# One-hot comparison of the token lists: 16-bit operands contiguous in the innermost dimension

## The chip, the cores and the metric

The kernel runs on one core of a Trainium2 chip. The metric is the time of one execution on the device, in microseconds (us); of several executions the median is given.

## What is computed

The program is a block of attention with a memory, a dense feed-forward layer and a mixture of 8 experts. The part around the change is the last one (the reference, cut):

```python
def _moe2_ref(x, w_gate, w1, w2):          # x: 2304 tokens x 512
    N, D = x.shape
    E = w_gate.shape[1]                    # 8 experts
    cap = N // E                           # 288 tokens each
    flat = (x @ w_gate).flatten()
    order = np.argsort(-flat)
    for idx in order:                      # best (token, expert) pair first
        tok, e = int(idx) // E, int(idx) % E
        if assigned[tok] >= 0 or counts[e] >= cap:
            continue
        assigned[tok] = e
        counts[e] += 1
    for e in range(E):
        mask = assigned == e
        h = np.maximum(x[mask] @ w1[e], 0.0)
        out[mask] = h @ w2[e]
```

Each expert thus gets exactly 288 tokens, and the kernel needs, for each expert, the list of its tokens' numbers, to gather their rows and later to scatter the results.

## The kernel before

**Stages.** Attention runs first (to about 370 us of the trace), interleaved with the first feed-forward pass; two more feed-forward passes follow (to about 728 us); then come the experts (class `Moe`). The routing decides one expert per phase: `phase` picks the expert that is full first, with a search of two times three stages (`search`). Each stage compares all tokens with 64 or 32 thresholds on VectorE (L847), counts by 18 matmuls on TensorE (L858), turns the counts into flags on VectorE (`fl`, L860), multiplies once more (L863) and reads the next base on VectorE (L867). After a phase the position of each of the expert's tokens is known (`self.pos`, `self.mem`), the expert's number goes to SyncE, which loads its weights (`wraw`, L1063), ScalarE and GpSimd split the weights into two parts (`convert`: L1073, and L1075 on GpSimd, whose two inputs and output lie in SBUF), and `lists` makes the list of tokens.

**The list (`lists`, L987).** Token n is row n mod 128, column t = n div 128 of an array of 128 x 18. A token's position among the 288 is cut into three thirds of 96 (`CW`): `j` is the third, `rb` the place in it plus 1, or 0 if the token is not the expert's. `rb` lies in `bank`, a tile of PSUM that holds most small arrays of the routing. L1006 compares, in two operations of 9 columns (`CUTS[3]` is 2), `rb` with the numbers 1 to 96 in `slot`, and writes the one-hot array `oh`, 16-bit, in which for each column t the 96 places follow one another. For each t a matmul (L1011) takes 128 places of `oh` as its weights (the last 32 belong to the next column or to the zeroed end, and their results are not read) and adds to 128 x 6 sums of token numbers in PSUM (`rs`, a single buffer that search and lists share). L1014 and L1016 make the index `idx`, and GpSimd gathers the rows in three indirect DMAs (`gather`, L1082).

**Order.** The instructions of TensorE go in program order, written out by hand with generators: `mlps` yields after each matmul of the experts, and `routes` is resumed between them after a count of such yields (`GAPS`). The other engines' order is chosen by a planner that works with estimated times. `lists` is itself a generator: it says before each piece whether VectorE ("v") or TensorE ("p") comes next, and `spare` (L973) resumes it at fixed places of the next phase's search: one "v" piece after each stage's comparisons, one "p" piece after a stage's last VectorE operation. For the list made during the third phase (`QUICK`) it is run through at once, and for the first list and the last two it is run to its end by `finish` (L1048), which gives `GAPS[8]` = 48 resumptions to other matmuls ahead of the "p" piece where there are such. TensorE first works on expert 0 after `LEAD` = 12 resumptions of the routing, that is after the second phase's search.

**Constants.** `slot` is an iota of 96 numbers made at the very start on GpSimd (L737, through `const`, L717). `open` (L760, in the timeline near 370 us) makes two zeroed buffers `oh` of 1760 elements on GpSimd (L770), used in turn.

Of the kernel before, what the change touches and what calls it, by code (L numbers as in the profile page):

```python
# [11 lines left out]
BF16 = mybir.dt.bfloat16  # L12
AF = mybir.ActivationFunctionType
OP = mybir.AluOpType
# [665 lines left out]
NE = 8  # L680
CAP = NT // NE
NTT = NT // 128
FE = 1024
KE = FE // 128
CW = CAP // 3
# [3 lines left out]
CUTS = (2, 2, 2, 2)  # L689
# [7 lines left out]
class Moe:  # L697
# [12 lines left out]
    def __init__(self, tc, pool):  # L710
        nc = self.nc = tc.nc
        self.tc = tc
        G, V = nc.gpsimd, nc.vector

        def const(shape, pattern, base, cm, name, dt=F32):
            t_ = pool.tile(shape, dt, name=name)
            G.iota(t_, pattern=pattern, base=base, channel_multiplier=cm, allow_small_or_imprecise_dtypes=True)  # L717
            return t_

        self.jt, self.jones, self.base8 = [], [], []  # L720
        for n, u in enumerate(self.UNITS):
            ts, os = [], []
            for r, st, o in zip(self.RS, self.ST, self.BASE):
                t_ = const([128, r], [[st, r]], o, 0, f"jt{n}_{st}")
                if u != 1.0:
                    V.tensor_scalar(t_, t_, u, None, op0=OP.mult)
                ts.append(t_)
                os.append(pool.tile([128, 128], BF16, name=f"jo{n}_{st}"))
                G.memset(os[-1], 0.0)
                G.memset(os[-1][0:r], st * u)  # L730
            self.jt.append(ts)
            self.jones.append(os)
            b_ = pool.tile([128, NE], F32, name=f"base{n}")
            V.memset(b_, -u * (self.ST[0] + self.ST[1] + 1))
            self.base8.append(b_)
        self.w8 = const([128, NE], [[-1, NE]], NE, 0, "w8")
        self.slot = const([128, CW], [[1, CW]], 1, 0, "slot", BF16)  # L737
        self.j3 = const([128, 3], [[1, 3]], 0, 0, "j3")
        tp = self.tp = pool.tile([128, NTT, 2], F32, name="tp")
        G.iota(tp[:, :, 0], pattern=[[128, NTT]], base=0, channel_multiplier=0, allow_small_or_imprecise_dtypes=True)  # L740
        G.iota(tp[:, :, 1], pattern=[[0, NTT]], base=0, channel_multiplier=1, allow_small_or_imprecise_dtypes=True)
        self.ones = pool.tile([128, 128], BF16, name="ones")
        V.memset(self.ones, 1.0)
        self.tri = pool.tile([128, 128], BF16, name="tri")
        G.affine_select(out=self.tri, in_=self.ones, pattern=[[1, 128]], compare_op=OP.is_gt, fill=0.0, base=0,
                        channel_multiplier=-1)
        self.later = pool.tile([128, 2, NTT], F32, name="later")
        V.memset(self.later, 1.0)
        V.memset(self.later[:, :, 0:1], 0.0)

        self.ab = [pool.tile([128, 2, NTT + 1], BF16, name=f"ab{i}") for i in range(2)]
        for t_ in self.ab:
            V.memset(t_, 0.0)

        self.room = pool.tile([128, NE], F32, name="room0")
        V.memset(self.room, float(CAP))
        self.code = pool.tile([128, NTT], F32, name="code0")
        V.memset(self.code, 0.0)

    def open(self, ctx, lg):  # L760

        tc, self.lg = self.tc, lg
        self.rt = ctx.enter_context(tc.tile_pool(name="mrt", bufs=2, reuse_waits="tile"))
        self.ri = ctx.enter_context(tc.tile_pool(name="mri", bufs=5, reuse_waits="tile"))
        kept = ctx.enter_context(tc.tile_pool(name="mrk", bufs=1, reuse_waits="tile"))

        def full(name, w):
            ts = [kept.tile([128, w], BF16, name=f"{name}{i}") for i in range(2)]
            for t_ in ts:
                tc.nc.gpsimd.memset(t_, 0.0)  # L770
            return itertools.cycle(ts)

        self.cmps, self.ohs, self.fls = full("cmp", 64 * (NTT + 1)), full("oh", CW * NTT + 128 - CW), full("fl", NE)
        self.p1 = ctx.enter_context(tc.tile_pool(name="mop1", bufs=1, space=PSUM, reuse_waits="tile"))


        bank, self.at = self.p1.tile([128, 512], F32, name="bank"), 0
        V = tc.nc.vector

        def small(*shape, dt=F32, at=None):  # L780
            n = 1
            for x in shape:
                n *= x
            o = self.at if at is None else at
            if at is None:
                self.at += n
            t_ = bank[:, o:o + n]
            if dt != F32:
                t_ = t_.bitcast(dt)
            if len(shape) == 2:  # L790
                t_ = t_.rearrange("p (a b) -> p a b", a=shape[0])
            return t_

        wide = self.at
        self.wv = small(NTT, NE)
        self.jh = small(NTT, 3, at=wide)
        (self.m, self.mw, self.lw, self.ac, self.px1, self.pos, self.take, self.mem,
         self.rb) = (small(NTT) for _ in range(9))
        self.key, self.hi, self.lo = (small(NTT, dt=I32) for _ in range(3))
        self.mg = small(2, NTT)  # L800
        self.cnt = small(2, NE)
        self.v, self.fe, self.nd, self.w8p = (small(NE) for _ in range(4))
        self.pens = [small(NE) for _ in range(2)]
        self.j3p, self.fmp, self.idf = small(3), small(1), small(3)
        assert self.at <= 512
        V.tensor_copy(self.w8p, self.w8)
        V.tensor_copy(self.j3p, self.j3)
        V.memset(self.pens[0], 0.0)
        self.pen = self.pens[0]
        self.stores, self.turn, self.ready, self.done, self.xs, self.hs = [], 0, [], 0, {}, {}  # L810
        self.split = {}
# [12 lines left out]
    def t18(self, nm, dt=F32):  # L824
        return self.rt.tile([128, NTT], dt, name=nm)
# [161 lines left out]
    def lists(self, i, raws):  # L987

        nc, V, two, t18 = self.nc, self.nc.vector, self.rt, self.t18
        yield "v"  # L990
        j, r, pos, rb, jh = t18("j"), t18("r"), self.pos, self.rb, self.jh
        V.tensor_scalar(j, pos, float(CW), None, op0=OP.is_ge)
        V.scalar_tensor_tensor(j, pos, float(2 * CW), j, op0=OP.is_ge, op1=OP.add)
        V.scalar_tensor_tensor(r, j, -float(CW), pos, op0=OP.mult, op1=OP.add)
        V.scalar_tensor_tensor(rb, r, 1.0, self.mem, op0=OP.add, op1=OP.mult)
        V.tensor_tensor(jh, j[:, :, None].to_broadcast([128, NTT, 3]),
                        self.j3p[:, None, :].to_broadcast([128, NTT, 3]), op=OP.is_equal)
        rhs = two.tile([128, NTT, 3, 2], BF16, name="rhs")
        V.tensor_tensor(rhs, jh[:, :, :, None].to_broadcast([128, NTT, 3, 2]),
                        self.tp[:, :, None, :].to_broadcast([128, NTT, 3, 2]), op=OP.mult)  # L1000
        wide = next(self.ohs)
        oh = wide[:, 0:CW * NTT].rearrange("p (t c) -> p t c", c=CW)
        n = NTT // CUTS[3]
        for t0 in range(0, NTT, n):
            yield "v"
            V.tensor_tensor(oh[:, t0:t0 + n], rb[:, t0:t0 + n, None].to_broadcast([128, n, CW]),  # L1006
                            self.slot[:, None, :].to_broadcast([128, n, CW]), op=OP.is_equal)
        yield "p"
        ps = self.p1.tile([128, 3, 2], F32, name="rs")
        for t in range(NTT):  # L1010
            nc.tensor.matmul(ps.rearrange("p a b -> p (a b)"), wide[:, CW * t:CW * t + 128],  # L1011
                             rhs[:, t].rearrange("p a b -> p (a b)"), start=(t == 0), stop=(t == NTT - 1))
        yield "v"
        V.tensor_reduce(self.idf[0:CW], ps[0:CW], axis=mybir.AxisListType.X, op=OP.add)  # L1014
        idx = self.ri.tile([CW, 3], I32, name="idx")
        V.tensor_copy(idx, self.idf[0:CW])  # L1016
        self.ready.append((self.split[i], idx, self.gather(idx)))
        if i == 0:
            with self.tc.issue_after(self.got):
                self.convert(i, raws[:3])  # L1020
            self.raws = raws[3:]
# [303 lines left out]
```

## Time and profile before

| | |
|---|---|
| time, median of 3 runs | 1027.81 us (1027.31 to 1028.85) |
| the profiled execution | 1039.62 us, its span 1037.9 us |
| TensorE (PE) busy | 941.3 us |
| VectorE (DVE) busy | 653.6 us |
| ScalarE (ACT) busy | 553.4 us |
| GpSimd (POOL) busy | 548.6 us |
| granted TensorE clock, mean | 0.960 of full |

The span goes from the first to the last instruction of the profiled execution. PEld is TensorE's loading of weights, which overlaps its matmuls. A row of a timeline gives the start and the time taken in us, the engine, the line, the operation, what it writes and reads, how many such in a row, and in brackets how long the engine had been idle before and what ended that.

### The profile page before, as it was taken

What the parts mean: (1) busy time and instruction counts of PE and PEld (TensorE: products, weight loads), DVE (VectorE), ACT (ScalarE), POOL (GpSimd) and SP (SyncE); (2) the same over time, 40 slices, a digit from 0 to 9 for tenths busy, and PEclk for the clock granted to TensorE, in tenths of its full rate; (3) what the DMA queues carried; (4) which work ended last, traced back from release to release, by engine and by line L of the source; (5) the groups of instructions that cost most, each with busy time, mean ns of one, the idle gap of its engine ahead of it and who ended that gap; (6) DMA issues with size and microseconds to landing.
All of it is one profiled execution on the core that took longest, in us unless ns stands there. A gap on an engine that the chain in (4) does not pass through costs nothing.

```text
span 1037.9 us, 19748 instructions
## 1 busy us (share of the span) xinstructions
PE 941.3 (91%) x7017; PEld 869.5 (84%) x7017; DVE 653.6 (63%) x1919; ACT 553.4 (53%) x1370; POOL 548.6 (53%) x555
## 2 busy tenths in 40 slices
PE   5787879999999989999999999999489898889996
PEld 4665768988899979999999999977388888889996
DVE  6899888788888727357426952326767677664110
ACT  6778878888888735344322333432343344335531
POOL 5666776667657546334322121211664876577841
PEclk8879889999999999999999999999699999999999
DMA  6445736364635277769684233101553355437410
GB/s 154 111 120 145 195 88 174 76 185 106 174 81 151 63 234 225 230 213 310 196 271 176 73 132 110 57 26 47 199 179 109 109 196 191 149 92 235 174 31 24
DMA packets 150723, 150.75 MB, mean 145 GB/s; under 512 B 71640, under 2 KB 122840, under 8 KB 150496
## 3 DMA queue, kind: packets, MB, share of 16 engines
q1 hardware_dynamic: 147552, 140.05, 44.1%
q0 software_dynamic: 3072, 9.44, 3.0%
q8 instruction: 55, 0.90, 0.4%
q14 instruction: 44, 0.36, 0.1%
HBM read 111.69 MB, written 37.77 MB: 144 GB/s over the span
## 4 chain that ended last, share of the span: by engine, by line
PE 61%; DVE 13%; issue 7%; DMA 6%; ACT 6%; POOL 3%; SPq 2%; another core or an unknown queue 0%; POOLq 0%; DVEq 0%; ACTq 0%
PE ph L1091 11%; PE ph L46 7%; PE ph L48 6%; PE ph L47 6%; PE py L46 4%; PE py L47 4%; PE py L48 4%; PE ps L313 3%; PE ps L218 2%; DMA xf<-x_d 2%; PE ps L272 2%; DVE cmp L847 2%; DMA wraw<-in_moe_w_dram 2%; PE rs L858 1%; PE ps L132 1%
## 5 line engine op out<-in xcount | busy, mean ns | idle before, releaser
L490 POOL TENSOR_TENSOR gf<-r 128x384 f32<-128x384 f32 (+1 forms) x108 | 87.4, 810 | 201.3 <-ACT r L488 191.1
L1075 POOL TENSOR_TENSOR wsp<-wraw,wsp 128x1024 fp32r<-128x1024 f32 x64 | 150.9, 2386 | 42.7 <-ACT wsp L1073 42.4
L27 DVE TENSOR_TENSOR gs<-gf,gs 128x384 fp32r<-128x384 f32 (+1 forms) x108 | 65.4, 605 | 92.0 <-ACT gs L26 91.4
L1091 PE MATMUL ph<-xs,wsp 128*128 128x288 f32 x768 | 120.0, 307 | 0.0
L1091 PEld LDWEIGHTS ph<-xs,wsp 128*128 128x128 f32 x768 | 107.9, 194 | 9.4 <-issue 9.2
L1091 PE MATMUL ph<-hs,wsp 128*128 128x288 f32 x768 | 114.5, 303 | 0.0
L247 POOL TENSOR_SCALAR P<-P,R,og 128x128 f32<-128x128 f32 (+2 forms) x144 | 100.3, 711 | 22.6 <-DVE R L245 18.4
L1091 PEld LDWEIGHTS ph<-hs,wsp 128*128 128x128 f32 x768 | 105.7, 191 | 0.7 <-DVE hs L1115 0.4
L1073 ACT ACTIVATE wsp<-wraw 128x1024 fp32r<-128x1024 f32 x64 | 64.2, 1051 | 52.4 <-DMA wraw<-in_moe_w_dram 31.4
L488 ACT ACTIVATE r<-ph 128x384 f32<-128x384 f32 (+1 forms) x108 | 48.6, 450 | 77.3 <-PE ph L48 76.1
L241 ACT ACTIVATE P<-P,R 128x128 f32<-128x128 f32 (+2 forms) x144 | 83.4, 581 | 9.3 <-DVE R L229 7.4
L26 ACT ACTIVATE gs<-gf 128x384 fp32r<-128x384 f32 (+1 forms) x108 | 52.5, 486 | 57.8 <-POOL gf L490 49.5
L46 PE MATMUL ph<-xt,win 128*128 128x384 f32 x240 | 81.3, 339 | 0.0
L47 PE MATMUL ph<-xt,win 128*128 128x384 f32 x240 | 80.8, 337 | 0.0
L48 PE MATMUL ph<-xt,win 128*128 128x384 f32 x240 | 80.7, 336 | 0.0
L46 PE MATMUL ph<-xs,win 128*128 128x288 f32 x192 | 64.6, 336 | 10.7 <-ACT r L488 7.9
L272 PE MATMUL ps<-ident,P 128*128 128x128 f32 x320 | 60.6, 296 | 8.3 <-POOL P L247 2.5
L47 PE MATMUL py<-gs,wout 128*128 128x384 f32 x192 | 64.9, 339 | 0.0
L27 DVE TENSOR_TENSOR ptb<-ps,ptb 128x384 fp32r<-128x384 f32 (+3 forms) x128 | 59.2, 464 | 8.1 <-ACT ptb L26 6.4
L48 PE MATMUL py<-gs,wout 128*128 128x384 f32 x192 | 64.0, 337 | 0.0
L229 DVE CUSTOM_DVE_ANT_0 P<-ps,maskw 128x128 f32<-128x128 f32 (+3 forms) x128 | 58.6, 484 | 8.0 <-PE ps L218 4.5
L46 PE MATMUL py<-gs,wout 128*128 128x384 f32 x192 | 63.5, 338 | 0.0
(264 smaller groups left out, 2595.1 us busy)
## 6 DMA issues: line engine op xcount, KB each, us to landing
wraw<-in_moe_w_dram SPq DMA_DIRECT2D x32, 1024.0 KB, 8.0
xt<-xs_d SPq DMA_DIRECT2D x12, 1536.0 KB, 7.1
x_d<-xo SPq DMA_DIRECT2D x32, 288.0 KB, 3.8
xf<-x_d SPq DMA_DIRECT2D x32, 288.0 KB, 3.9
xs_d<-xs SPq DMA_DIRECT2D x8, 1152.0 KB, 6.8
raw<-in_moe_w_in_dram SPq DMA_DIRECT2D x16, 512.0 KB, 5.3
raw<-in_moe_w_out_dram SPq DMA_DIRECT2D x16, 512.0 KB, 4.4
yp<-yo SPq DMA_DIRECT2D x32, 144.0 KB, 4.5
```

The costliest lines, as they stand in the source:

```text
L27: (eng or nc.vector).tensor_tensor(lo, src, hi.bitcast(F32), op=OP.subtract)
L46: nc.tensor.matmul(out, lhi, rhi, start=start, stop=False)
L47: nc.tensor.matmul(out, lhi, rlo, start=False, stop=False)
L48: nc.tensor.matmul(out, llo, rhi, start=False, stop=stop)
L229: nc.vector.tensor_tensor_reduce(out=pw, in0=ps[:, 0:W[u]], in1=maskw[:, 512 - 128 * t:640], op0=OP.add, op1=OP.min, scale=-0.125, scalar= ...
L241: nc.scalar.activation(pw, pw, AF.Exp, bias=R[:, 0, u:u + 1], scale=-1.0, accum_out=R[:, 1, u:u + 1])
L247: nc.gpsimd.tensor_scalar(PP[n][w], PP[n][w], R[:, 2, w:w + 1], og9[:, hp, w:w + 1], op0=OP.mult, op1=OP.mult)
L272: nc.tensor.transpose(tr[:, 128 * i:128 * i + 128], P[:, 128 * i:128 * i + 128], ident)
L490: nc.gpsimd.tensor_tensor(gf, r, r, op=OP.mult)
L1073: nc.scalar.activation(w[:, 0, hs], raw[:, hs], AF.Copy)
L1075: eng.tensor_tensor(w[:, 1, hs], raw[:, hs], w[:, 0, hs].bitcast(F32), op=OP.subtract)
L1091: nc.tensor.matmul(out, l[a], r[b], start=i + p == 0, stop=i == n - 1 and p == 2)
```

## The change

`rb` becomes a 16-bit tile in SBUF. `slot` becomes a constant of 96 x 18 16-bit elements, in which each number stands 18 times in a row; it is made in `open`. `oh` is laid out as 128 places of 18 columns, with one buffer in place of two, and is filled by one comparison in place of two: 96 x 18 elements with the columns innermost, so that all three operands step by one element there. `lists` gives back control once less. The matmul of column t takes as weights the elements t, t + 18, t + 36, ... of `oh`, 36 bytes apart.

```diff
--- before.py
+++ after.py
@@ -734,7 +734,6 @@
             V.memset(b_, -u * (self.ST[0] + self.ST[1] + 1))
             self.base8.append(b_)
         self.w8 = const([128, NE], [[-1, NE]], NE, 0, "w8")
-        self.slot = const([128, CW], [[1, CW]], 1, 0, "slot", BF16)
         self.j3 = const([128, 3], [[1, 3]], 0, 0, "j3")
         tp = self.tp = pool.tile([128, NTT, 2], F32, name="tp")
         G.iota(tp[:, :, 0], pattern=[[128, NTT]], base=0, channel_multiplier=0, allow_small_or_imprecise_dtypes=True)
@@ -764,13 +763,16 @@
         self.ri = ctx.enter_context(tc.tile_pool(name="mri", bufs=5, reuse_waits="tile"))
         kept = ctx.enter_context(tc.tile_pool(name="mrk", bufs=1, reuse_waits="tile"))
 
-        def full(name, w):
-            ts = [kept.tile([128, w], BF16, name=f"{name}{i}") for i in range(2)]
+        def full(name, w, n=2):
+            ts = [kept.tile([128, w], BF16, name=f"{name}{i}") for i in range(n)]
             for t_ in ts:
                 tc.nc.gpsimd.memset(t_, 0.0)
             return itertools.cycle(ts)
 
-        self.cmps, self.ohs, self.fls = full("cmp", 64 * (NTT + 1)), full("oh", CW * NTT + 128 - CW), full("fl", NE)
+        self.slot = kept.tile([128, CW, NTT], BF16, name="slot")
+        tc.nc.gpsimd.iota(self.slot, pattern=[[1, CW], [0, NTT]], base=1, channel_multiplier=0,
+                          allow_small_or_imprecise_dtypes=True)
+        self.cmps, self.ohs, self.fls = full("cmp", 64 * (NTT + 1)), full("oh", 128 * NTT, 1), full("fl", NE)
         self.p1 = ctx.enter_context(tc.tile_pool(name="mop1", bufs=1, space=PSUM, reuse_waits="tile"))
 
 
@@ -988,7 +990,7 @@
 
         nc, V, two, t18 = self.nc, self.nc.vector, self.rt, self.t18
         yield "v"
-        j, r, pos, rb, jh = t18("j"), t18("r"), self.pos, self.rb, self.jh
+        j, r, rb, pos, jh = t18("j"), t18("r"), t18("rb", BF16), self.pos, self.jh
         V.tensor_scalar(j, pos, float(CW), None, op0=OP.is_ge)
         V.scalar_tensor_tensor(j, pos, float(2 * CW), j, op0=OP.is_ge, op1=OP.add)
         V.scalar_tensor_tensor(r, j, -float(CW), pos, op0=OP.mult, op1=OP.add)
@@ -998,17 +1000,13 @@
         rhs = two.tile([128, NTT, 3, 2], BF16, name="rhs")
         V.tensor_tensor(rhs, jh[:, :, :, None].to_broadcast([128, NTT, 3, 2]),
                         self.tp[:, :, None, :].to_broadcast([128, NTT, 3, 2]), op=OP.mult)
-        wide = next(self.ohs)
-        oh = wide[:, 0:CW * NTT].rearrange("p (t c) -> p t c", c=CW)
-        n = NTT // CUTS[3]
-        for t0 in range(0, NTT, n):
-            yield "v"
-            V.tensor_tensor(oh[:, t0:t0 + n], rb[:, t0:t0 + n, None].to_broadcast([128, n, CW]),
-                            self.slot[:, None, :].to_broadcast([128, n, CW]), op=OP.is_equal)
+        wide = next(self.ohs).rearrange("p (c t) -> p c t", t=NTT)
+        yield "v"
+        V.tensor_tensor(wide[:, 0:CW], rb[:, None, :].to_broadcast([128, CW, NTT]), self.slot, op=OP.is_equal)
         yield "p"
         ps = self.p1.tile([128, 3, 2], F32, name="rs")
         for t in range(NTT):
-            nc.tensor.matmul(ps.rearrange("p a b -> p (a b)"), wide[:, CW * t:CW * t + 128],
+            nc.tensor.matmul(ps.rearrange("p a b -> p (a b)"), wide[:, :, t],
                              rhs[:, t].rearrange("p a b -> p (a b)"), start=(t == 0), stop=(t == NTT - 1))
         yield "v"
         V.tensor_reduce(self.idf[0:CW], ps[0:CW], axis=mybir.AxisListType.X, op=OP.add)
```

## Rows read from the trace of the kernel before

**Rows 1.** Page, part 1: busy us, share of the span, instructions of each engine.
```profile
PE 941.3 (91%) x7017; PEld 869.5 (84%) x7017; DVE 653.6 (63%) x1919; ACT 553.4 (53%) x1370; POOL 548.6 (53%) x555
```

**Rows 2.** Stages: length; PE, PEld, DVE, ACT, POOL busy (x); PEclk, DMA share, GB/s.
```profile
728.00:750.00 22.00, 7.81 (x139) 5.49 (x138) 15.75 (x52) 6.78 (x8) 16.62 (x9) 0.61 0.67 230
750.00:1038.00 288.00, 260.70 (x2438) 250.18 (x2438) 148.73 (x551) 117.29 (x209) 179.19 (x104) 0.97 0.40 134
```

**Rows 3.** Chain that ended last, list 0: start us, us, what.
```profile
728.97 1.94 DVE oh L1006 x2
...
730.96 0.42 PE rs L1011 x10
...
731.76 0.22 DVE la L877
```

**Rows 4.** Timeline of PE, then of POOL, at list 1.
```profile
767.84 0.36 PE L1011 MATMUL rs<-rhs,oh 128*128 128x6 bf16 x8 [1.59 <-DVE oh L1006]
...
764.99 9.36 POOL L1075 TENSOR_TENSOR wsp<-wraw,wsp 128x1024 fp32r<-128x1024 f32 x4 [7.40 <-ACT wsp L1073]
```

**Rows 5.** Tile oh: count, duration ns min/median/max, first and last start, forms.
```profile
L1011 PEld LDWEIGHTS <-oh x144: 95/96/101, 730.0 to 945.6; 128*128 128x128 bf16 x144
...
L1006 DVE TENSOR_TENSOR oh<-bank,slot x16: 1046/1048/1049, 728.9 to 942.9; 128x864 bf16<-128x864 f32 x16
```

**Rows 6.** Timeline: weight loads of list 0, comparisons of list 1.
```profile
730.96 0.32 PEld L1011 LDWEIGHTS <-oh 128*128 128x128 bf16 x10 [0.70 <-DVE oh L1006]
...
766.74 2.01 DVE L1006 TENSOR_TENSOR oh<-bank,slot 128x864 bf16<-128x864 f32 x2
```

**Rows 7.** DVE: a form's busy us, mean ns; a line's ns, min/median/max.
```profile
L27 DVE TENSOR_TENSOR xs<-tr,xs 128x288 fp32r<-128x288 f32 x32 | 13.8, 452 | 22.2 <-ACT xs L26 22.2
...
L38 DVE TENSOR_SCALAR gf<-r x20: 387/692/991, 30.8 to 417.6; 128x512 int32<-128x512 int32 x20
```

**Rows 8.** Loads of four-byte weights by form: count, busy us, mean ns, idle before.
```profile
L664 PEld LDWEIGHTS pr<-two,lt 128*128 128x128 f32 x36 | 5.6, 189 | 0.3
...
L652 PEld LDWEIGHTS pr<-ys,wgs 128*16 128x16 f32 x48 | 4.4, 94 | 6.1 <-DVE ys L27 2.3 <-ACT ys L26 1.4 <-ACT yr L675 0.5
```

**Rows 9.** Timeline of DVE and POOL near 69 us; durations of L177.
```profile
69.50 1.78 DVE L177 SCALAR_TENSOR_TENSOR qp<-nq,e 128x640 f32<-128x640 f32 x1
...
69.05 1.54 POOL L163 TENSOR_TENSOR vt<-nv,vt 128x640 fp32r<-128x640 f32 x1
...
L177 DVE SCALAR_TENSOR_TENSOR qp<-nq,e x16: 811/826/2131, 8.7 to 339.3; 128x640 f32<-128x640 f32 x16
```

**Rows 10.** POOL from 750 to 945 us by line: busy us, mean ns, idle before.
```profile
L1075 POOL TENSOR_TENSOR wsp<-wraw,wsp 128x1024 fp32r<-128x1024 f32 x44 | 103.7, 2386 | 39.7 <-ACT wsp L1073 39.6
```

**Rows 11.** Timeline of DVE and POOL at lists 3 and 5.
```profile
837.37 1.05 DVE L1006 TENSOR_TENSOR oh<-bank,slot 128x864 bf16<-128x864 f32 x1
...
836.38 4.77 POOL L1075 TENSOR_TENSOR wsp<-wraw,wsp 128x1024 fp32r<-128x1024 f32 x2 [2.18 <-ACT wsp L1073]
...
905.74 1.05 DVE L1006 TENSOR_TENSOR oh<-bank,slot 128x864 bf16<-128x864 f32 x1
...
905.07 4.76 POOL L1075 TENSOR_TENSOR wsp<-wraw,wsp 128x1024 fp32r<-128x1024 f32 x2 [8.39 <-ACT wsp L1073]
```

**Rows 12.** Timeline of PE: waits for a gather, a reduction, a flag.
```profile
823.42 0.55 PE L1103 MATMUL tr<-ident,xg 96*128 96x96 f32 x4 [0.31 <-DMA xg<-y_d,idx]
...
845.66 0.59 PE L858 MATMUL rs<-hot,cmp 128*128 128x8 bf16 x18 [0.57 <-DVE bank L1014]
...
886.04 0.17 PE L863 MATMUL rs<-fl,jo 128*128 128x8 bf16 x1 [2.89 <-DVE fl L860]
```

**Rows 13.** POOL's constants by form: count, busy us, mean ns, idle before.
```profile
L770 POOL MEMSET oh<- 128x1760 bf16 x2 | 3.1, 1566 | 0.0
...
L717 POOL IOTA jt<- 128x32 f32 x4 | 0.6, 149 | 0.0
...
L717 POOL IOTA slot<- 128x96 bf16 x1 | 0.2, 245 | 0.0
```

## The prediction

> **What bounds the kernel now.** I read the busy sums first, then a table by stages, then the chain that ended last around the changed lines, then the waits of TensorE (PE) there, then the rows of the changed operations. PE is busy for 91% of the span, VectorE (DVE) for 63%, GpSimd (POOL) for 53% [rows 1]. The stages differ [rows 2]. From 750 to 1038 us PE works 260.7 of 288 us, nearly throughout. Between 728 and 750 us it works 7.8 of 22 us: there the routing of the experts is one serial chain of DVE and PE. The changed code runs eight times, once per expert, between 728 and 946 us; I call the runs list 0 to list 7. At list 0 the chain goes through the changed lines without a gap: the two comparisons, 10 matmuls, a reduction, the index, and then the next phase's first operation [rows 3]. What is saved or lost there arrives whole at 750 us, since the following phase hangs on it. At list 1 PE stands still for the comparison, 1.59 us ahead of the first half alone [rows 4]. At lists 6 and 7 DVE compares while PE works on through expert matmuls. At lists 2 to 5 the halves lie in the shadow of PE, but directly ahead of the flags (`fl`, L860) that PE needs next, with little to spare.
>
> **The comparison, DVE.** Now: 2 operations of 864 elements, 1.046 to 1.049 us each [rows 5], a pair 2.01 us [rows 6]. After: one of 1728 elements, all operands 16-bit. If it makes two results per cycle it has 864 steps, like one of the two today: 1.05 us. If one, it costs a second 864 at the slope between two rows, (1.048 - 0.452)/(864 - 288) = 1.03 ns each [rows 5, 7]: 1.94 us. No two-source row of before runs at two per cycle; the nearest is a one-source operation of 512 elements with durations from 387 to 692 ns, so the engine has such a rate [rows 7]. I take 1.05: a saving of 0.96 us where the pair is on the path. [...]
>
> **The matmuls behind it.** Today 8 of the 18 run under the second half; the other 10 follow it, about 25 ns apart, (0.32 - 0.096)/9 [rows 5, 6]. After, all 18 follow: 8 x 25 = +0.20 us wherever PE waits for the comparison.
>
> **Weights 36 bytes apart.** Each of the 144 loads now reads neighbouring 2-byte weights; after, one word in 18. No row of before has that. A load of 128 four-byte columns takes 189 ns, of 16 columns 94 ns: 0.85 ns per column and about 80 ns fixed. A load of 128 two-byte columns takes 96 ns, some 15 ns above the fixed part [rows 5, 8]. So two-byte weights go in seven times as fast, in less than the 25 ns that separate the loads. Lower bound: nothing. Upper bound from the rows: the rate of the four-byte loads, 128 x 0.85 = 108 ns each, 83 ns more than the spacing now. I stay near the row of the same type and take a doubling of the 15 ns to 30, that is +5 ns per load: 0.09 us per list. [...]
>
> **A wait that is new.** Today one source of the comparison lies in the PSUM bank (`self.rb`), and all 16 take the same time whatever POOL does [rows 5]. After, both lie in SBUF. Rows show what that does: at 69.50 us an operation of DVE with two SBUF sources takes 1.78 us in place of 0.81 because POOL's began at 69.05 and ends at 70.59; over the trace this form goes from 811 to 2131 ns [rows 9]. POOL's weight split (L1075) has the same two-SBUF-source form and takes 2.39 us; between 750 and 945 us it covers 103.7 of 195 us, 53% [rows 10]. So a comparison meets one half of the time and waits 1.19 us on average: 0.63 us. Queued behind it on DVE are the flags and hence PE (L863). By list: list 0 meets none, since POOL's work in that stretch [rows 2] is the gathers, which need this list, and the splits queued behind them. List 1 at 766.74 meets the run from 764.99, whose first split ends at 767.33: +0.59 [rows 4, 6]. Lists 2 to 5: bounds 0 and, where a comparison of before starts inside a split, the remainder of that split: 1.40 us at list 3 (838.77 - 837.37), 0.78 at list 4, 1.71 at list 5 (907.45 - 905.74), together 3.89 (the first and the last of the three stand in [rows 11]). I take 4 x 0.63 = 2.5 and let half of it reach the end, 1.27, because PE also waits 2.89 us at 886.04 for a flag while no comparison runs, and such waits take up part of a delay [rows 12]. Lists 6 and 7: nothing, since `finish` puts 48 resumptions of the experts' matmuls between comparison and list. POOL loses up to 1 us per meeting; it idles 39.6 us there for ScalarE [rows 10], so nothing.
>
> **One step fewer.** With one operation in place of two, matmuls, reduction and the three gathers of lists 2 to 6 come one search stage earlier, and POOL's gathers move ahead of two or so splits, in the same total. PE's wait for a gather was 0.31 us, its wait for the reduction at 845.66 us 0.57 [rows 12]. Bounds 0 and -0.88; I take -0.31. List 7 has no search left to move past.
>
> **Constants.** The 245 ns iota leaves the start, where the chain then runs through SP's queue and DMAs: nothing. At 372 us POOL loses two memsets of 1.566 us [rows 13] and gains one of 2304 elements (2.05 us at the same rate) and an iota of 1728 elements (245 ns for 96, 149 for 32, so up to 2.7 us): up to +1.6 us ahead of L475. PE there waits for ScalarE and DMAs, not for POOL: I take 0 and keep 1.6 as the upper bound. A single `oh` buffer costs nothing: list 0's last load starts by 731.4 us, list 1's comparison at 766.74.
>
> **Sum.** List 0: -0.96 + 0.20 + 0.09 = -0.67. List 1: -0.67 + 0.59 = -0.08. Lists 2 to 7, loads: 6 x 18 x 5 ns = +0.54. Lists 2 to 5, waits for POOL: +1.27. Earlier step: -0.31. Together +0.75 us. The profiled run took 1039.62 us for a span of 1037.9, 1.1% above the median of 1027.81; I add the difference to the median: 1028.6. A measurement of this kernel can tell 0.2%, 2.1 us, from no change, so this is no change. Own range: -2.4 (no waits, free loads, the whole 0.88) to +5.3 (3.89 in full, nothing earlier, POOL's 1.6): 1025.4 to 1033.1.
>
> **Rivals.**
> 1. The gain is clean: waits for POOL vanish in PE's slack and loads cost nothing: -0.76 - 0.76 - 0.88 = -2.4, 1025.4. For it: lists 0 and 1 are on the path beyond doubt. Against: the 53%.
> 2. Each weight costs an access of its own, twice slower again: 60 ns per load, 35 over the spacing, 30 over my value: 144 x 30 = +4.3, 1032.9. [...]
> 3. Slower outright: strided weights lose the fast path and load like four-byte ones. Place: the 18 loads of each list, in PE's queue ahead of the next search matmuls, at lists 2 to 7 in a PE that has no room. Price: 83 - 5 = 78 ns x 144 = +11.2, 1039.8. It decides from about 13 ns per load on, where 144 loads eat the 1.8 us that the earlier step and lists 0 and 1 give. For it: the rows have fast loads for contiguous weights only.
> 4. The comparison doesn't get its rate: 1.94 us, 0.89 more at lists 0 and 1 and, half recovered, at lists 2 to 5: 4 x 0.89 = +3.6, 1032.1.
>
> **Chances.** Forecast 0.52 (faster 0.05, same 0.35, slower 0.12), rival 1 0.15, rival 2 0.14, rival 3 0.12, rival 4 0.07. So faster 0.20, same 0.35, slower 0.45, and the likeliest single case lies within 0.2%. The range 1025.2 to 1034.0 leaves out rival 3 and thin tails.
>
> **What would show it.** Right: one comparison per list near 1.05 us at list 0, longer by the remainder of a split where POOL is in one; L1011 loads some 30 ns apart; the chain from the start of list 0's comparison to the next phase's first operation 0.7 us shorter than 2.79 us (731.76 - 728.97) [rows 3]. Wrong: comparisons of 1.9 us with POOL idle (rival 4); loads 60 or 100 ns apart (rivals 2, 3); no long comparison in spite of splits (rival 1). Another order of DVE's instructions in the expert stage would upset lists 2 to 5.

## The result, and the profile of the changed kernel

The changed kernel takes 1039.78 us (median of 11, 1031.94 to 1045.89); the kernel before, timed beside it, 1029.16 us (11, 1027.31 to 1034.72). The comparison puts the ratio at 1.0082, 95% interval 1.0059 to 1.0105 (the two medians alone would give 1.0103): slower by 0.0082 x 1029.16 = 8.4 us, and the median is outside the range of the prediction (1025.2 to 1034.0). Two later comparisons of the same two kernels gave 1.0098 (1.0068 to 1.0128) and 1.0082 (1.0053 to 1.0110). All results below are ratios to runs of the kernel before made in the same batch, because batches differ: the kernel before took 1029 us here, 1031 us on average with e1 to e4, and 1041 to 1044 us in the others. The transfers of expert weights differ too: a median of 5.4 to 5.8 us in the profiles of e1 to e4, 7.1 to 9.6 in all the others, the changed kernel's (7.2) among them. DMA issues of the kernel before (its profile ahead of the prediction, an execution of 1039.62 us) and of e3 (count, KB, median us to landing):

```profile
wraw<-in_moe_w_dram SPq DMA_DIRECT2D x32, 1024.0 KB, 8.0
```

```profile
wraw<-in_moe_w_dram SPq DMA_DIRECT2D x32, 1024.0 KB, 5.6
```

So the spans of two profiles from different batches are not compared. An expectation below puts this down to the chip; but the record has chip 0 both for e1 to e4 (1031 us) and for e17 and e18 (1044 us), so what differs stays open.

The changed operations, by tile: count, ns min/median/max, first and last start, forms. First the kernel after:

```profile
L1009 PEld LDWEIGHTS <-oh x144: 139/162/167, 732.7 to 947.6; 128*128 128x128 bf16 x144
L1009 PE MATMUL rs<-rhs,oh x144: 165/202/224, 732.7 to 947.6; 128*128 128x6 bf16 x144
L1005 DVE TENSOR_TENSOR oh<-rb,slot x8: 1050/1052/2611, 731.4 to 943.0; 128x1728 bf16<-128x1728 bf16 x8
```

Against [rows 5] the comparison does twice the elements in the same 1.05 us, but for 2.61 at list 1 and 1.94 at list 6. The weight load went from 96 to 162 ns. How far the loads of one list lie apart is read from PE's timeline (start, length, idle time before, and who ended it); list 2 and list 4 after, then list 2 before:

```profile
809.22 1.22 PE L1009 MATMUL rs<-rhs,oh 128*128 128x6 bf16 x18 [0.26 <-DVE nb L869]
...
878.86 1.22 PE L1009 MATMUL rs<-rhs,oh 128*128 128x6 bf16 x18 [2.31 <-DVE nb L869]
```

```profile
809.71 0.59 PE L1011 MATMUL rs<-rhs,oh 128*128 128x6 bf16 x18 [0.27 <-DVE nb L867]
```

That is (1.22 - 0.20)/17 = 60 ns from one matmul to the next, and (0.59 - 0.165)/17 = 25 ns before. The stages after, as in [rows 2]:

```profile
728.00:750.00 22.00, 11.21 (x151) 8.34 (x150) 16.48 (x65) 5.75 (x7) 11.85 (x8) 0.72 0.73 234
750.00:1040.00 290.00, 268.75 (x2453) 258.46 (x2450) 146.25 (x550) 119.39 (x212) 187.14 (x106) 0.94 0.40 134
```

In the expert stage PE is busy 8.1 us longer and its granted clock is 0.94 in place of 0.97. A part of that goes with the execution and not with the kernel: in later profiles PE of the kernel before is busy for 262.9 and 263.5 us from 750 us on, at 0.96 and 0.95 (e5, e9), and PE of the changed kernel for 273.5 and 267.0 us, at 0.93 and 0.96 (e10, e17). At 0.96 the two kernels are 4.1 us apart (e5, e17).

At list 0, DVE's order has changed. Timeline of DVE, after and then before:

```profile
730.49 0.17 DVE L994 TENSOR_SCALAR j<-bank 128x18 f32<-128x18 f32 x1
...
731.44 1.05 DVE L1005 TENSOR_TENSOR oh<-rb,slot 128x1728 bf16<-128x1728 bf16 x1
732.41 0.26 DVE L1001 TENSOR_TENSOR rhs<-bank,tp 128x108 bf16<-128x108 f32 x1
732.66 0.69 DVE L638 TENSOR_TENSOR yr<-py,yr 128x512 f32<-128x512 f32 x1
734.05 0.17 DVE L1012 TENSOR_REDUCE bank<-rs 96x3 f32<-96x6 f32 x1 [0.70 <-PE rs L1009]
734.25 0.16 DVE L1014 CAST idx<-bank 96x3 int32<-96x3 f32 x1
734.33 0.29 DVE L879 TENSOR_TENSOR la<-lg,bank 128x144 f32<-128x144 f32 x1
```

```profile
726.09 0.17 DVE L992 TENSOR_SCALAR j<-bank 128x18 f32<-128x18 f32 x1
...
727.18 0.27 DVE L999 TENSOR_TENSOR rhs<-bank,tp 128x108 bf16<-128x108 f32 x1
728.28 0.69 DVE L638 TENSOR_TENSOR yr<-py,yr 128x512 f32<-128x512 f32 x1 [0.83 <-PE py L48]
...
731.68 0.29 DVE L877 TENSOR_TENSOR la<-lg,bank 128x144 f32<-128x144 f32 x1
```

Before, DVE waited 0.83 us for the last dense matmul and compared behind L638. After, the planner put the comparison ahead of `rhs` and L638, into that gap. From `j` to `la` list 0 takes 734.33 - 730.49 = 3.84 us, before 5.59: 1.75 us gained, where the prediction had 0.67. In e4 below, which has one comparison too but reads PSUM, it stays behind L638, so the missing step alone does not move it.

List 1 meets the split on GpSimd, as predicted. DVE, POOL and PE after:

```profile
768.37 2.61 DVE L1005 TENSOR_TENSOR oh<-rb,slot 128x1728 bf16<-128x1728 bf16 x1
```

```profile
767.69 5.53 POOL L1073 TENSOR_TENSOR wsp<-wraw,wsp 128x1024 fp32r<-128x1024 f32 x2 [6.52 <-ACT wsp L1071]
```

```profile
771.58 1.23 PE L1009 MATMUL rs<-rhs,oh 128*128 128x6 bf16 x18 [2.19 <-DVE rhs L1001]
```

The comparison takes 1.56 us more while the first split runs, and `rhs`, now behind it, keeps PE waiting: 2.19 us, as long as the two waits of the kernel before at this list together (1.59 and 0.61).

### The profile page after: what moved, and what is told of

The parts are those of the page before. It is cut to its first block, busy times and chain, and to the rows that moved or that the text cites. A ratio compares the mean times of both kernels' runs of the same rounds, so it can differ in the third digit from the quotient of the medians.

```text
span 1040.0 us, 19737 instructions
## 1 busy us (share of the span) xinstructions
PE 952.6 (92%) x7017; PEld 881.7 (85%) x7017; DVE 651.0 (63%) x1911; ACT 553.1 (53%) x1370; POOL 550.7 (53%) x554
## 4 chain that ended last, share of the span: by engine, by line
PE 65%; DVE 12%; ACT 6%; issue 6%; DMA 6%; POOL 3%; SPq 2%; POOLq 0%; DVEq 0%; ACTq 0%
PE ph L1089 14%; PE ph L46 7%; PE ph L47 6%; PE ph L48 6%; PE py L46 4%; PE py L47 4%; PE py L48 4%; PE ps L313 3%; PE ps L218 3%; PE ps L272 2%; DMA xf<-x_d 2%; PE rs L860 2%; DMA wraw<-in_moe_w_dram 1%; ACT P L241 1%; PE ps L132 1%
## 5 line engine op out<-in xcount | busy, mean ns | idle before, releaser
L1089 PEld LDWEIGHTS ph<-xs,wsp 128*128 128x128 f32 x768 | 110.6, 198 | 0.2
L272 PE MATMUL ps<-ident,P 128*128 128x128 f32 x320 | 62.9, 305 | 8.6 <-DVE R L229 3.0
```

The costliest lines, as they stand in the source:

```text
L272: nc.tensor.transpose(tr[:, 128 * i:128 * i + 128], P[:, 128 * i:128 * i + 128], ident)
L1089: nc.tensor.matmul(out, l[a], r[b], start=i + p == 0, stop=i == n - 1 and p == 2)
```

## The experiments

Theory A: the strided loads are the loss. Rivals: B, GpSimd (the comparison's waits for it, 2.61 us in place of 1.05 at list 1 above, which two expectations call locks, and the constants at 372 us); C, the missing step of `lists`; later S against T, whether a strided load costs more than the time it adds to PE's queue.

### The layout of the one-hot turned alone

```diff
-        wide = next(self.ohs)                                            # e1, on the kernel before
-        oh = wide[:, 0:CW * NTT].rearrange("p (t c) -> p t c", c=CW)
+        wide = next(self.ohs).rearrange("p (c t) -> p c t", t=NTT)
+        oh = wide[:, 0:CW].rearrange("p c t -> p t c")
...
-            nc.tensor.matmul(ps.rearrange("p a b -> p (a b)"), wide[:, CW * t:CW * t + 128],
+            nc.tensor.matmul(ps.rearrange("p a b -> p (a b)"), wide[:, :, t],
...
-        wide = next(self.ohs).rearrange("p (c t) -> p c t", t=NTT)       # e2, on the kernel after
+        wide = next(self.ohs)
+        oh = wide[:, 0:CW * NTT].rearrange("p (t c) -> p c t", c=CW)
...
-            nc.tensor.matmul(ps.rearrange("p a b -> p (a b)"), wide[:, :, t],
+            nc.tensor.matmul(ps.rearrange("p a b -> p (a b)"), wide[:, CW * t:CW * t + 128],
```

> The kernel before with one thing changed: the comparison writes [column, token group], so the weights lie 36 bytes apart; two comparisons of 864 from PSUM, steps and constants as before (one buffer of 2304 in place of two of 1824). Theory A (the strided loads are the main part of the loss): loads 162 ns and about 61 ns apart against 25, 144 x 36 ns = 5.2 us, nearly all on PE's path: ratio 1.004 to 1.006. Theory B (the loads hide in PE's slack, the loss is GpSimd's: longer comparisons and the constants): ratio within 0.001 of 1. The comparisons themselves should stay at 1.05 us; if the strided write slows them to 1.9 us, add up to 3 us to either.

> The changed kernel with one thing taken back: the comparison writes [token group, column], so the weights are contiguous again. 16-bit operands, one operation, wide column numbers, all constants and steps stay as changed. The write is now strided by 192 bytes in the innermost dimension. Theory A: loads at 96 ns and 25 ns apart, 5.2 us come back: ratio to the kernel before about 1.003 if the comparison keeps 1.05 us, up to 1.006 if it falls to 1.9 us. Theory B: nothing comes back, ratio about 1.008.

Measured: 1.0516 (1.0480 to 1.0552) and 1.0632 (1.0602 to 1.0663). Both lie far above every expectation, and neither tells A from B, because the comparison became the loss; the loads were near what was expected (medians 163 ns in e1, 104 in e2). Tile `oh` in e1, then in e2:

```profile
L1006 DVE TENSOR_TENSOR oh<-bank,slot x16: 3835/3932/4142, 724.6 to 977.7; 128x864 bf16<-128x864 f32 x16
```

```profile
L1006 DVE TENSOR_TENSOR oh<-rb,slot x8: 8496/8556/10352, 730.7 to 995.7; 128x1728 bf16<-128x1728 bf16 x8
```

VectorE writes 2-byte elements 36 bytes apart at 3932/864 = 4.6 ns each, 192 bytes apart at 5.0 ns, and next to each other at 1048/864 = 1.2 ns with the operands of e1 [rows 5] and 1052/1728 = 0.6 ns with those of e2 (the changed kernel). So whoever lays `oh` out in one order and wants it in the other pays more here, 2 x (3.93 - 1.05) = 5.8 us per list in e1 and 8.56 - 1.05 = 7.5 us in e2, than the loads cost: 18 x 35 ns = 0.63 us.

### Weights 4 and 12 bytes apart

The one-hot is stored in groups of g columns; inside a group the layout is that of the changed kernel. The comparison keeps its innermost contiguous runs (of g), the weights lie 2g bytes apart, and 96 x g column numbers are made at the start.

```diff
+        g, wide = 2, next(self.ohs)        # e3: 2, e7: 6
+        oh = wide[:, 0:CW * NTT].rearrange("p (a c b) -> p a c b", c=CW, b=g)
...
+        V.tensor_tensor(oh, rb.rearrange("p (a b) -> p a b", b=g)[:, :, None, :].to_broadcast([128, NTT // g, CW, g]),
+                        self.slot[:, None, :, :].to_broadcast([128, NTT // g, CW, g]), op=OP.is_equal)
```

> The changed kernel with weights 4 bytes apart in place of 36: the one-hot is stored [9 groups, 96 columns, 2], the column numbers are 96 x 2 from the start of the program, the large constant of 1728 is gone. [...] Then 5.2 us of loads and about 2 us of GpSimd's constants come back: ratio 0.999 to 1.002. Theory B (GpSimd's locks are the loss): lock waits stay, ratio about 1.004 to 1.006. If any step at all takes loads off the fast path: spacing 61 ns as in the changed kernel, ratio 1.005 or more.

> As the run with pairs (weights 4 bytes apart), but with groups of six: weights 12 bytes apart, column numbers 96 x 6 from the start. [...] Theory A2 (the price comes only beyond some larger distance): loads 96 ns, ratio 1.001 as with pairs.

Measured: e3 1.0011 (0.9991 to 1.0031), e7 1.0042 (1.0016 to 1.0069). The loads of e3, then of e7:

```profile
L1010 PEld LDWEIGHTS <-oh x144: 96/96/103, 733.1 to 943.1; 128*128 128x128 bf16 x144
...
L1005 DVE TENSOR_TENSOR oh<-rb,slot x8: 1049/1052/2490, 731.8 to 939.2; 128x1728 bf16<-128x1728 bf16 x8
```

```profile
L1010 PEld LDWEIGHTS <-oh x144: 124/144/148, 730.5 to 958.0; 128*128 128x128 bf16 x144
...
843.01 0.96 PE L1010 MATMUL rs<-rhs,oh 128*128 128x6 bf16 x18 [0.29 <-DVE nb L868]
```

At 4 bytes a load costs what a contiguous one costs (96 ns), at 12 bytes 144 ((0.96 - 0.187)/17 = 46 ns from matmul to matmul), at 36 bytes 162. The comparison keeps 1.05 us with runs of two. So the price is there at 12 bytes already: theory A2's 96 ns and 1.001 both fail in e7. The times of e3 and e7, from two batches, agree with the loads: e3 lies within the 0.999 to 1.002 expected. Why 12 bytes cost more than 4 is not shown.

### The kernel before with one step, and with the constants alone

```diff
-CUTS = (2, 2, 2, 2)
+CUTS = (2, 2, 2, 1)                        # e4
...
+        tc.nc.gpsimd.iota(self.slots.rearrange("p (t c) -> p t c", c=CW), pattern=[[0, NTT], [1, CW]], base=1, ...)   # e6, in open
```

> The kernel before with one comparison of 1728 elements (from PSUM, 1.9 us expected) in place of two of 864, and so one step less per list; contiguous weights, no 16-bit operand. Theory A: the order of the steps matters little, ratio 0.999 to 1.002 (lists 0 and 1 lose 0.2 us each, since all 18 matmuls follow the comparison). Theory C (the earlier step of the lists itself costs PE time in the expert stage, by the order of the search matmuls and the gathers): ratio 1.003 or more.

> The kernel before with the constants of the changed kernel alone: the column numbers are made by one operation of 1728 elements at 372 us (not used beyond the first 96) in place of 96 at the start, one buffer of 2304 zeros in place of two of 1760. Comparison, weights and steps as before. Theory K (GpSimd's extra 2 to 4 us at 372 us delay what stands behind them and reach the end): first matmuls after 410 us come 2 us later, ratio 1.002. Theory of the prediction (hidden): ratio 1.000.

Measured: e4 1.0077 (1.0049 to 1.0106); e6 1.0004 (0.9984 to 1.0024). No cost of the constants can be told, within 2.5 us; e6's column numbers take 1.68 us, those of 3.25 us stand in e11 below. One undivided comparison of 1.95 us costs 0.8%, above theory A's 0.999 to 1.002: at list 3 of e4 it stands ahead of a flag, and PE waits for it, where the kernel before has no such wait.

```profile
839.70 1.94 DVE L1006 TENSOR_TENSOR oh<-bank,slot 128x1728 bf16<-128x1728 f32 x1
...
841.92 0.14 DVE L860 TENSOR_TENSOR fl<-rs,room 32x8 bf16<-32x8 f32 x1
```

```profile
842.12 0.17 PE L863 MATMUL rs<-fl,jo 128*128 128x8 bf16 x1 [1.03 <-DVE fl L860]
```

e3 has the same one step with 1.05 us and, in the same batch, 0.0066 +- 0.0035 (95%, as all ranges of this form) less: 6.8 us, near 8 x 0.9 = 7.2 us of comparison. So the step alone is not what costs. That the length counts in full at every list is not shown: e3 differs from e4 in the layout, the operands and the order on DVE as well, and PE's waits for flags at lists 2 to 5 of e4 (1.56, 1.03, 2.12 and 1.35 us) are only 2.3 us longer in sum than in the profile of the kernel before (3.76). Where the rest of e4's 8 us arises stays open.

### Two steps again

```diff
-        yield "v"
-        V.tensor_tensor(wide[:, 0:CW], ...)
+        for c0 in range(0, CW, CW // 2):    # e12; e8: the same with pairs, 960 and 768 elements
+            yield "v"
+            V.tensor_tensor(wide[:, c0:c0 + CW // 2], ...)
```

> As the run with pairs, but with two comparisons (960 and 768 elements, about 0.6 and 0.5 us) and the two steps of the kernel before. Theory C (the missing step costs several us, since the matmuls and gathers of a list come a search stage earlier; the run with one step and nothing else was 0.8% slower): the quicker comparison is then a plain gain, ratio 0.994 to 0.998. Theory D (what cost there was the undivided comparison of 1.95 us standing in one piece ahead of the flags, not the step): ratio 0.999 to 1.002, like the run with pairs and one step.

> The changed kernel with two comparisons of 864 (0.6 us each) and the two steps of the kernel before; the stride, the 16-bit operands and the constants stay. Theory A: the stride stays and so does the loss, within 0.003 of the changed kernel's ratio in this batch. Theory C (one step fewer puts a list's matmuls and gathers a search stage earlier and that costs): ratio 0.004 or more below the changed kernel's.

Measured: e8 1.0039 (1.0014 to 1.0063), above both expectations; e12 1.0090 (1.0062 to 1.0119), like the changed kernel beside it (1.0098). That speaks against theory C, but the test is not clean. The planner put both halves behind one another all the same, ahead of `rhs`, and the pair can take long: 3.29 us at list 3 of e12, where the median of one is 0.60. That GpSimd's split is the cause, as at list 1 above, is the author's estimate. DVE and then PE there:

```profile
842.95 3.29 DVE L1007 TENSOR_TENSOR oh<-rb,slot 128x864 bf16<-128x864 bf16 x2
846.17 0.26 DVE L1001 TENSOR_TENSOR rhs<-bank,tp 128x108 bf16<-128x108 f32 x1
...
846.91 0.85 PE L860 MATMUL rs<-hot,cmp 128*128 128x8 bf16 x18 [2.65 <-DVE cmp L849]
```

PE waits 2.92 us in the same way at list 5, and 4.64 us at list 1 in place of e10's 2.16; e10 has no such wait at lists 3 and 5. So a gain by the second step could be hidden here. e8 has the same wait at list 3 (2.65 us), which may be a part of its 0.4%; nothing was run to tell. What does tell is that e3 above and e11 below have one step and are level with the kernel before: the missing step is not the changed kernel's loss. Whether it costs a microsecond or two that list 0's gain covers is not shown.

### The changed kernel with and without the stride, in one batch

e11 is the changed kernel with pairs and with all its constants (those of 1728 elements are made and not used): everything but the 36 bytes.

> The kernel before, unchanged: a second profile of it. The first profiled execution (1039.62 us) lies above all timed ones, so a comparison stage by stage against it can mislead. Ratio 1.000 within 0.002; profiled time 1028 to 1034 us; the place where the two profiles differ is the part of the first one that isn't typical. Every theory expects the same here.

> The kernel before, unchanged, for one profile on the same chip as the three runs sent with it: chips differ (1030 us on one, 1044 us on another, with the 1 MB transfers of expert weights taking 5.6 us on the first and 8.0 us on the second), so stages are to be compared on one chip only. Every theory expects the same here.

> The changed kernel, unchanged, beside the runs sent with it. Ratio 1.006 to 1.010 if the first result holds on this chip too; below 1.004 if the loss depends on how fast the chip delivers the expert weights.

> The changed kernel with its weights 4 bytes apart, everything else kept: one comparison, 16-bit operands, the operation of 1728 column numbers and the buffer of 2304 at 372 us (the column numbers used are 96 x 2 from the start). Theory A (the stride is the main part of the loss): loads 96 ns and 25 ns apart; the ratio lies 0.005 (144 x 36 ns = 5.2 us) below that of the changed kernel in this batch. Theory B (the step, the locks and the constants are the loss): it lies within 0.002 of it.

> The base of e13 and e14 on their chip: changed kernel with weights 4 bytes apart. Theory A: ratio 0.998 to 1.002, as in the first run of it (0.9995).

Measured: the kernel before against itself 0.9991 (0.9969 to 1.0013, e5); e9, one execution for its profile, 1042.81 us; e10 1.0098 (1.0068 to 1.0128); e11 0.9995 (0.9972 to 1.0019), again as e15 0.9996 (0.9972 to 1.0021). Theory A holds, B falls: without the stride nothing of the loss is left, though e11's comparison meets GpSimd at list 1 even longer (3.13 us) and its PE waits at list 4 as in the changed kernel (2.11 us). The loads of e11:

```profile
L1013 PEld LDWEIGHTS <-oh x144: 96/97/107, 725.5 to 940.5; 128*128 128x128 bf16 x144
```

The three comparisons of the changed kernel average 1.0086 +- 0.0015 (weighted by their intervals), the two of the base 0.9996 +- 0.0017: the stride is worth 0.0091 +- 0.0023, 9.5 +- 2.4 us. The loads themselves add 144 x 35 ns = 5.0 us to PE's queue. PE in the same stretch (columns as in [rows 2]), e11 and then e10:

```profile
750.00:1030.00 280.00, 255.38 (x2407) 244.21 (x2405) 140.06 (x524) 114.41 (x203) 178.25 (x102) 0.98 0.41 138
```

```profile
750.00:1030.00 280.00, 260.00 (x2346) 249.56 (x2346) 146.08 (x549) 115.31 (x203) 182.40 (x102) 0.93 0.41 136
```

These two profiles differ in the granted clock, too (0.98 and 0.93); over all executions the gap is smaller, 0.952 for e11 and 0.949 for e10.

### Is it PE's time alone, and at which lists?

```diff
+        for t in range(26):                 # e13, on e11: 26 x 25 ns, contiguous weights, zeros
+            nc.tensor.matmul(ps.rearrange("p a b -> p (a b)"), self.ones, self.zero, start=False, stop=(t == 25))
...
+        if i < 2:                           # e14, on e11: 36 bytes apart at lists 0 and 1 alone
```

> The run with pairs and the constants (weights 4 bytes apart, ratio 0.9995) with 26 more matmuls behind the 18 of each list, contiguous weights times zeros, added to the same sums: 26 x 25 ns = 0.65 us of TensorE per list, as much as 18 x 36 ns of strided loads. Theory T (what costs is TensorE's time in the lists, and the granted clock and the waits follow from it): the whole loss comes back, ratio 0.007 to 0.011 above the base e15. Theory S (the stride costs something beyond the loads' time): only 5 us or less, ratio 0.003 to 0.005 above the base.

> As the base e15, but lists 0 and 1 with weights 36 bytes apart, the others 4 bytes apart. If a load costs the same wherever it stands: 36 x 36 ns = 1.3 us, a quarter, ratio 0.001 to 0.003 above the base. If the loss arises in the expert stage, where PE has no room (lists 2 to 7): ratio within 0.001 of the base. If it arises on the serial chain at lists 0 and 1: ratio 0.005 or more above.

> The changed kernel, beside e18 on one chip. Ratio 1.007 to 1.011, as in its two earlier comparisons (1.0082 and 1.0098). Theory S (the stride costs more than the loads' time): 0.003 or more above e18. Theory T (only TensorE's time counts): within 0.002 of e18.

> Weights 4 bytes apart and 26 matmuls with contiguous weights more per list (0.65 us of TensorE per list, no stride), beside e17 on one chip. Theory T: ratio within 0.002 of e17's. Theory S: 1.005 or less, 0.003 or more below e17.

Measured: e13 1.0054 (1.0025 to 1.0083), e18 (the same kernel) 1.0054 (1.0029 to 1.0078), e17 (the changed kernel) 1.0082 (1.0053 to 1.0110); e14 1.0011 (0.9988 to 1.0035). PE at list 2 of e13; with the padding it ends at 803.30 us, without at 802.61, 0.69 us earlier:

```profile
802.00 0.61 PE L1015 MATMUL rs<-rhs,oh 128*128 128x6 bf16 x18 [0.28 <-DVE nb L873]
802.47 0.83 PE L1018 MATMUL rs<-zero,ones 128*128 128x6 bf16 x26
```

Padding costs 0.0058 +- 0.0026 over the base, 6.1 +- 2.7 us, for 8 x 0.65 to 0.69 = 5.2 to 5.5 us of PE: within the interval, PE's time in the lists reaches the end in full. It lies between what theories T (0.007 to 0.011) and S (0.003 to 0.005) expected. At lists 0 and 1 alone the stride costs 0.0015 +- 0.0034, which agrees with a quarter of 5.0 us and with a quarter of 9.5; at the upper end (5.1 us) it would be half of the loss, so that does not place it. Between the changed kernel and the padded one lie 0.0028 +- 0.0038 where both ran in one batch, 0.0032 +- 0.0024 with all runs; the expectations of e17 and e18 were 0.003 or more (S) and 0.002 or less (T), so that pair decides nothing. About 5 us of the loss are thus the loads' time; the other 4 or so come with the stride too, by e10 and e11, but by what way is not settled. A lower clock goes with it: mean 0.949 for the changed kernel (e10, e17), 0.950 and 0.952 for the padded one, 0.952 for the base, 0.954 to 0.957 for the kernel before in these batches; within the batch of e9 to e12 an execution is 0.5 us longer per 0.001 less clock. Whether the clock is the cause there was not tried.

### The quick comparison where it is on the path

```diff
+        if i < 2:                           # e16, on the kernel before: pairs and one operation at lists 0 and 1
```

> The quick comparison (16-bit, weights 4 bytes apart, one operation) at lists 0 and 1 alone, where it lies on the path; the other six as in the kernel before, with small constants. Theory of the prediction (lists 0 and 1 gain about 0.7 us each, nothing else changes): ratio 0.998 to 0.9995. If the comparison's new place in VectorE's order ahead of rhs gives the 2 to 3 us that list 0 gained in the profiles: 0.996 to 0.998. Rival (clock and waits take it back): 1.000 or above.

Measured: 0.9976 (0.9949 to 1.0003), the lowest of all, 2.5 us below the kernel before, though its interval still touches 1. It is in line with list 0's gain. Whether the other six lists have anything to gain from the quick comparison is not shown: e11 and e15, which have it at all lists, lie 0.0020 above e16, within the intervals.

## Why the prediction was wrong

- **The loads: the step that failed.** The prediction saw the four-byte rate (+83 ns), saw that a step was in no row, and took "+5 ns per load", a doubling of the 15 ns that the columns seemed to take. Measured: +66 ns of load, +35 ns of spacing, seven times the term: 5.0 us in place of 0.7. The +5 ns was the author's estimate, and no run shows it. What failed is how it was made: it carried the fixed 80 ns of the four-byte loads over to the two-byte ones, left 15 ns to be slowed, and found the doubled 30 only 5 above the spacing of 25. Rival 2 had the price, 35 ns over the spacing, and 0.14 of the chance; that each weight costs an access of its own, as it says, is not shown. The runs give the time of a load by the distance of its weights alone: 96 ns at 2 and at 4 bytes (the kernel before, e3), 144 at 12 (e7), 162 at 36 (the changed kernel). At 36 bytes it stayed under the 189 ns of the four-byte loads [rows 8].
- **Rival 3** (the four-byte rate, 1039.8) gives exactly the measured median, by luck: its price is wrong, 83 ns of spacing in place of 35.
- **The size.** Even rival 2, at +4.3 us, is short of the 8.4 measured: it let a load cost its spacing and nothing more. The stride's full effect is 9.5 +- 2.4 us; by what way about 4 us of it arise stays open, as said.
- **The comparison** takes the 1.05 us taken: right. (The row of one-source operations it leaned on runs from 387 to 991 ns, not to 692 [rows 7].) Rival 4's 3.6 us for a comparison of 1.94 us looks too low, by the 6.8 us between e4 and e3; but those two differ in more than the length.
- **Waits for GpSimd.** Right in kind. Predicted 0.59 us at list 1 and 1.27 at lists 2 to 5; measured 1.56 at list 1, none at lists 2 to 5 (1.050 to 1.052 each) and 0.89 at list 6, where nothing waits. The sum came out near (1.86 against 1.56), by luck: its places did not. The planner moved the comparison ahead of `rhs` and `cmp`, and at lists 3 to 5 it now begins before GpSimd's splits, at list 3 by only 0.11 us (841.00 and 841.11). The prediction named another order as what would upset lists 2 to 5.
- **List 0** gained 1.75 us, not 0.67: the comparison no longer stands behind `rhs` and L638. By the prediction's own sign, from the comparison's start to `la`, it is 2.89 us (734.33 - 731.44) and not 0.7 below 2.79, since those two now stand in between. With pairs list 0 gains 0.67 more (e11).
- **One step fewer** was to bring 0.31: e10 and e12 differ by 0.0008 +- 0.0041, far too wide to see that. At list 4 PE waits 2.31 us for the search base that stands ahead of the list's matmuls, at the same list before 0.26 us; e11 has that wait too, so it is not the stride's.
- **Constants**: nothing that could be told (e6, e11), as predicted, though the column numbers took 3.25 us and not at most 2.7.
- **The sum without the loads** was +0.75 - 0.72 = +0.03 us, and the change without the stride measured 0.9996 +- 0.0017, -0.4 +- 1.8 us: right, but partly by luck, since errors cancel (list 0's gain, list 4's wait).

## What to carry to other kernels

Before a layout is turned to please one engine, price the other engine that reads it: here VectorE won 1 us per list (one comparison of 1.05 us in place of two), and TensorE's 18 loads of the list lost 0.63 us each time in a queue that had little room (busy for 260.7 of 288 us [rows 2]). When the cost of an access pattern is in no row, give the pessimistic bound from the rows a good part of the chance, instead of taking a value near the favourable row: here the bounds were 0 and 83 ns, 5 was taken, and 35 measured. And look for the layout between the two: with runs of two 16-bit elements VectorE still compared 1728 elements in the 1.05 us that 864 took before, and TensorE's loads took 96 ns as before (e3).

## What the runs showed of the hardware that was not expected

- 16-bit weight loads of 128 columns by distance: 2 and 4 bytes 96 ns (25 ns from load to load; 104 ns at 2 bytes in e2), 12 bytes 144 (46), 36 bytes 162 (60).
- VectorE's 16-bit writes at a large step: 4.6 ns per element at 36 bytes, 5.0 at 192, against 1.2 and 0.6.
- GpSimd's column numbers cost by pattern and not only by count. The changed kernel, 18 equal numbers in a row, then e6, runs of 96 ascending ones:

```profile
372.36 3.25 POOL L773 IOTA slot<- 128x1728 bf16 x1
```

```profile
L773 POOL IOTA slot<- 128x1728 bf16 x1 | 1.7, 1677 | 0.0
```
